# DMA transposes one block earlier, loads one chunk further ahead, and more half FFN steps as filler, in a fused attention and SwiGLU kernel

## The chip, the cores and the metric

The kernel runs on one core of a Trainium2 chip. The metric is device time in microseconds (us), the median of several executions. A program on one core has no second die to compare with, so a run counts as slow only if it is over 1.5% above the fastest run of the same kernel. Three different chips were used for the three rounds of experiments, and the kernel before was timed beside them each time; the median of its fast runs was 367.4, 368.1 and 369.65 us there. Absolute times are compared within one round, and ratios across rounds.

The readings call the engines by short names: PE (TensorE), PEld (its weight loads), DVE (VectorE), ACT (ScalarE), POOL (GpSimd), SP (SyncE, which here only issues DMAs). The granted clock is the share of full speed that the throttle of TensorE allowed, so 0.5 is half clock; a dip is a stretch in which it is below 1. A wait, a landing time or a start is that of the one execution that was profiled.

## The reference, cut to what matters

```python
# q, k, v: (8 batches, 8 heads, 576 positions, 64);  window 64, causal
scores = q @ k.T / 8;  masked to 0 <= i - j < 64;  softmax
attn_out = softmax(scores) @ v            # per batch and head
x = attn_out as (4608 tokens, 512)
g = x @ w_gate                            # 512 x 1536
out = (silu(g) * (x @ w_val)) @ w_out     # 1536 x 512
```

The kernel works in 36 chunks of 128 tokens for attention and 9 groups of 512 tokens (four chunks) for the FFN.

## The kernel before

Every operation is recorded in program order with what it reads and writes. The recorder then gives each engine its own queue in that order and adds semaphore waits for data (a write before a read) and for buffers (a read before the next write). DMAs are recorded on the queue of the engine that issues them: loads on GpSimd, transposes and output stores on SyncE. A queue is in order: a DMA that has to wait holds up those recorded after it.

In the code below the calls are abridged and "..." marks cuts; the line numbers are those that the profile gives.

```python
NQ = 6       # buffers for q and k chunks as loaded
NV = 10      # for v
NZ = 4       # buffers for transposed q (qT); kT keeps all chunks

def TD(self, n):                 # transposes of k and q of chunk n, by DMA
    g.op("sp", dma_start_transpose(kT[n], kn[n % NQ]), ...)      # L363
    g.op("sp", dma_start_transpose(qT[n % NZ], qn[n % NQ]), ...) # L366
def XD(self, n):                 # transpose of the attention output of chunk n
    g.op("sp", dma_start_transpose(xT[...], xb[n % 4]), ...)     # L490
def A(self, n, nxt):             # attention-value matmuls of n; S(nxt) in the middle
def S(self, n):                  # score matmuls of n: need kT[n], qT[n]   (L394)
def F(self, c, f, t0=0, t1=512): # one FFN step (128 of the 1536 columns) of group c
def O(self, c, u):               # output tile u of group c, its store on SP
def T(self, n):                  # transposes of k and q by the PE (first chunks), L350
...
    self.F(0, 4, 0, 256)
    for f in range(5):
        self.F(0, f, 256, 512)
    self.T(4)
    ...
    self.S(8)
    self.O(0, 0)

    def block(n):
        load(n + 4)              # q, k, v of chunk n+4, on POOL
        self.A(n, n + 1)
        self.XD(n)               # not for n = 11
        self.TD(n + 2)
    place = {(1, 1, 0): 8, (1, 1, 2): 9, (1, 2, 1): 10, (1, 3, 0): 11, ...}
    # (group, output tile, step) -> block; from group 3 on one block for each output tile
```

The softmax here doesn't subtract the row's maximum and nothing guards it: scores larger than these inputs give would overflow.

Of the kernel before, what the change touches and what calls it, by code (L numbers as in the profile page):

```python
# [10 lines left out]
NCH = T // 128  # L11
# [138 lines left out]
class _Kernel:  # L150
# [423 lines left out]
    def build(self):  # L574
        W = lambda a, b: (self.load_w("g", a, b), self.load_w("v", a, b))

        def load(n):
            if n < NCH:
                self.load_qk(n)
                self.load_v(n)  # L580

        self.first_loads()
        self.init()
        self.load_v(0)
        self.init_pool_a()
        self.load_v(1)
        self.init_mask(self.nmask, "nmask", -30000.0)
        W(0, 1)
        self.load_qk(2)
        W(1, 2)  # L590
        self.load_qk(3)
        self.load_v(2)
        self.load_v(3)
        W(2, 4)
        self.init_mask(self.mask, "mask", 0.0)
        self.init_va(4, self.NV, "pool")
        for f in range(4, 12, 2):
            W(f, f + 2)
        for n in range(4, 8):
            load(n)  # L600

        self.banks("a", [5, 6, 7, 4, 0, 1])
        self.warm(13)
        self.first_cast("k", None, "dve")
        self.first_cast("q", 0, "act")
        self.first_cast("q", 1, "dve")
        tk = self.first_T("k")
        tq = self.first_T("q")
        b0, b1 = self.bias(0), self.bias(1)
        self.warm(2)  # L610
        for n in range(2):
            self.first_ev("k", n, "dve", *tk)
            self.first_ev("q", n, "act", *tq)
        self.S(0, b0)
        self.S(1, b1)
        self.warm(4)
        self.A(0)
        self.warm(2)
        self.A(1)
        self.warm(1)  # L620
        self.X(0, "act")
        self.warm(3)
        self.X(1, "act")
        self.warm(2)
        self.banks("a", [5, 6, 7, 4])
        self.F(0, 0, 0, 256)
        self.F(0, 1, 0, 256)
        self.T(2, "dve")
        self.T(3, "dve")
        load(8)  # L630
        b2 = self.bias(2)
        self.S(2, b2)
        b3 = self.bias(3)
        self.S(3, b3)
        self.F(0, 2, 0, 256)
        self.A(2)
        self.A(3)
        self.F(0, 3, 0, 256)
        self.X(2, "act")
        self.X(3, "act")  # L640
        self.F(0, 4, 0, 256)
        self.load_wo(0, 6)
        self.load_wo(6, 12)
        load(9)

        for f in range(5):
            self.F(0, f, 256, 512)
        self.T(4)
        load(10)
        self.F(0, 5)  # L650
        self.S(4)
        self.T(5)
        load(11)
        self.F(0, 6)
        self.A(4, 5)
        self.F(0, 7)
        self.T(6)
        self.X(4, "act")
        self.F(0, 8)
        self.A(5, 6)  # L660
        self.F(0, 9)
        self.X(5, "act")
        self.T(7)
        self.F(0, 10)
        self.A(6, 7)
        self.TD(8)
        self.F(0, 11)
        self.X(6, "act")
        self.F(1, 0, 0, 256)
        self.A(7)  # L670
        self.TD(9)
        self.F(1, 1, 0, 256)
        self.F(1, 2, 0, 256)
        self.X(7, "act")
        self.F(1, 3, 0, 256)
        for f in range(4):
            self.F(1, f, 256, 512)
        self.S(8)
        self.O(0, 0)

        def block(n):
            if n >= NCH:
                return
            load(n + 4)
            self.A(n, n + 1 if n + 1 < NCH else None)
            if n != 11:
                self.XD(n)
            if n + 2 < NCH:
                self.TD(n + 2)

        place = {(1, 1, 0): 8, (1, 1, 2): 9, (1, 2, 1): 10, (1, 3, 0): 11,
                 (2, 0, 0): 12, (2, 1, 0): 13, (2, 1, 2): 14, (2, 2, 1): 15, (2, 3, 0): 16}
        for n in range(17, NCH):
            place[(n - 5) // 4, (n - 5) % 4, 0] = n
        for c in range(1, NFC):
            for u in range(int(c == 1), 4):
                late = c == NFC - 1 and u == 3
                for s in range(3):
                    if (c, u, s) != (1, 1, 0):
                        self.F(c, 3 * u + s)  # L700
                    if s != 1 and (c, u, s) in place:
                        block(place[c, u, s])
                    if s == 1 and not late:
                        self.O(c - 1, u)
                        if (c, u) == (1, 3):
                            self.X(11, "act")
                    if s == 1 and (c, u, s) in place:
                        block(place[c, u, s])
                if late:
                    self.O(c - 1, u)  # L710
        for u in range(3):
            self.O(NFC - 1, u)
        self.O_last(NFC - 1, 3)
        self.g.emit()
# [42 lines left out]
```

## Time and profile before

| | before |
|---|---|
| time, median (the four runs beside the changed kernel) | 369.46 us |
| span of the profiled run | 369.7 us |
| PE busy | 328.5 us, 89% |
| PE waiting for "DMA qT<-qn" | 23.1 us in 11 waits |
| PE waiting for the first k chunk to transpose itself (T(4)) | 2.8 us |
| mean granted PE clock | 0.982 |

From the page of the kernel before: busy time, then two rows of the span in 40 equal slices (9.2 us each), a digit being tenths.

```profile
PE 328.5 (89%) x3428; PEld 166.3 (45%) x3467; DVE 213.3 (58%) x459; ACT 138.9 (38%) x249; POOL 112.7 (30%) x151
...
PE   7986998856699766999999998999899999999997
...
PEclk9999999899699998999999999999999999999999
```

PE has holes between the seventh and the sixteenth slice (roughly 60 to 150 us), and the granted clock has dips in the same places. From 260 us on it is full.

The waits of PE in the kernel before (line and what it waited for: total us, number, longest):

```profile
PE ps L394 <- DMA qT<-qn: 23.1, 11, 4.3
...
PE ps L350 <- DMA kn<-in_k_dram: 2.8, 1, 2.8
```

L394 is S, L350 is T. Next, the timeline of PE (start, duration, group of instructions; in brackets the idle time before it and what ended it), at S(9), S(10), S(11), S(12) and the first FFN matmuls after the last of them:

```profile
65.93 0.54 PE L394 MATMUL ps<-qT,kT 64*64 64x128 bf16 x21 [2.13 <-DMA qT<-qn]
...
78.17 0.41 PE L394 MATMUL ps<-qT,kT 64*64 64x128 bf16 x21 [3.67 <-DMA qT<-qn]
...
86.78 0.41 PE L394 MATMUL ps<-qT,kT 64*64 64x128 bf16 x21 [1.64 <-DMA qT<-qn]
...
95.50 0.64 PE L394 MATMUL ps<-qT,kT 64*64 64x128 bf16 x24 [4.34 <-DMA qT<-qn]
...
96.70 1.49 PE L508 MATMUL ps<-xT,Wg 128*128 128x512 bf16 x3 [0.33 <-DVE rc L458]
97.98 1.91 PE L508 MATMUL ps<-xT,Wv 128*128 128x512 bf16 x4
```

Four waits of 2.1, 3.7, 1.6 and 4.3 us stand within 30 us. After the last, a group of three gate matmuls of 512 columns took 1.49 us instead of 0.81, and a group of four value matmuls 1.91 us instead of 1.03. The Trainium skill, "TensorE: Matmul & The Clock Gate", Part 1, says that the clock falls to half after an idle window of about 3.4 us, that the window runs freely, and that the number of slow matmuls therefore varies from run to run. This trace agrees in kind: the granted clock is 0.67 in the stretch 90 to 100 us.

The queue of SP in the same stretch shows why S(10) is late:

```profile
67.98 1.20 SPq L490 DMA_TRANSPOSE xT<-xb  x1
69.23 1.26 SPq L363 DMA_TRANSPOSE kT<-kn  x1
70.53 1.90 SPq L366 DMA_TRANSPOSE qT<-qn  x1
```

These are the x transpose of block 8, then the k and q transposes of chunk 10. The q transpose was issued from 70.5 us on and landed 7.5 us later (the landing time that the view of this tile gives for this window), which is when S(10) started, at 78.2 us. Block 9, which holds S(10), came straight after.

From 259.9 to 302.55 us, with no loads left, five chunks took 42.65 us: 8.53 us each is PE's own pace.

### The profile page before, as it was taken

The page shows a single profiled execution, that of the slowest core. Times are in us where ns is not written, and L with a number is a line of the kernel's source. Part 1 is how long each engine was busy: PE and PEld are TensorE (multiplying, and loading weights), DVE is VectorE, ACT ScalarE, POOL GpSimd, SP SyncE. Part 2 cuts the span into 40 slices and gives each one's busy share as a digit, 9 for nine tenths or more (in the row PEclk, how much of TensorE's full clock was granted, in tenths as well). Part 3 has the DMA queues.
Part 4 walks back from the last instruction along what each step waited for, and adds up shares of the span by engine and source line. Part 5 has one row for each costly group of instructions (what it writes and reads, how often), then busy time and mean ns, then how long its engine had stood idle before and what let it go on. Part 6 is the DMA issues. An engine that isn't in the chain of part 4 may idle for free.

```text
span 369.7 us, 8222 instructions
## 1 busy us (share of the span) xinstructions
PE 328.5 (89%) x3428; PEld 166.3 (45%) x3467; DVE 213.3 (58%) x459; ACT 138.9 (38%) x249; POOL 112.7 (30%) x151
## 2 busy tenths in 40 slices
PE   7986998856699766999999998999899999999997
PEld 3555556323344333444444444444444444444444
DVE  4455897355366643666666665666566666445530
ACT  2553854323143331443333433333334442232321
POOL 7999964222502242222222242222000000000000
PEclk9999999899699998999999999999999999999999
DMA  9999999999968999999999999999423221101003
GB/s 171 157 176 169 169 175 154 170 115 126 121 75 89 128 124 83 120 111 125 125 116 128 133 101 125 127 119 85 102 73 73 73 73 43 44 28 57 30 29 113
DMA packets 169909, 40.26 MB, mean 109 GB/s; under 512 B 156432, under 2 KB 165392, under 8 KB 169872
## 3 DMA queue, kind: packets, MB, share of 16 engines
q0 software_dynamic: 117312, 18.36, 72.0%
q1 hardware_dynamic: 51376, 20.72, 30.6%
q10 hardware_dynamic: 1184, 0.66, 0.6%
q8 instruction: 27, 0.44, 0.5%
q14 instruction: 10, 0.08, 0.1%
HBM read 37.75 MB, written 9.44 MB: 128 GB/s over the span
## 4 chain that ended last, share of the span: by engine, by line
PE 33%; issue 31%; POOL 19%; DMA 14%; SPq 1%; DVE 1%; ACT 0%; POOLq 0%
PE ps L508 19%; PE ps L532 12%; DMA qT<-qn 6%; POOL qn L263 6%; POOL va L325 5%; DMA va<-in_v_dram 5%; POOL kn L263 3%; DMA kn<-in_k_dram 3%; POOL Wg L331 1%; POOL Wv L331 1%; PE ps L443 1%; PE ps L394 1%; SPq L363 1%; PE ps L561 1%; SPq L490 1%
## 5 line engine op out<-in xcount | busy, mean ns | idle before, releaser
L516 DVE SCALAR_TENSOR_TENSOR uu<-sig,ps 128x512 bf16<-128x512 bf16 (+1 forms) x117 | 75.3, 644 | 99.4 <-ACT sig L514 98.9
L508 PE MATMUL ps<-xT,Wv 128*128 128x512 bf16 (+1 forms) x467 | 114.1, 367 | 0.1
L508 PE MATMUL ps<-xT,Wg 128*128 128x512 bf16 (+1 forms) x435 | 107.4, 367 | 5.8 <-issue 4.5
L532 PE MATMUL ps<-Wo,hT 128*128 128x512 bf16 x417 | 95.8, 380 | 0.3 <-issue 0.2
L514 ACT ACTIVATE sig<-ps 128x512 bf16<-128x512 f32 (+1 forms) x117 | 66.1, 565 | 61.4 <-PE ps L508 61.1
L518 DVE SCALAR_TENSOR_TENSOR hT<-uu,ps 128x512 bf16<-128x512 bf16 (+1 forms) x117 | 75.5, 645 | 4.6 <-PE ps L508 0.5
L263 POOL DMA_DIRECT2D qn<-in_q_dram x38 | 34.5, 922 | 134.1 <-DMA qT<-qn 133.9
L508 PEld LDWEIGHTS ps<-xT,Wv 128*128 128x128 bf16 x468 | 46.3, 99 | 49.4 <-issue 3.2
L532 PEld LDWEIGHTS ps<-Wo,hT 128*128 128x128 bf16 x420 | 41.2, 98 | 49.9 <-issue 1.0
L508 PEld LDWEIGHTS ps<-xT,Wg 128*128 128x128 bf16 x468 | 42.8, 99 | 42.3 <-issue 1.6
L404 ACT ACTIVATE pt<-ps 128x512 bf16<-128x512 f32 x72 | 38.9, 595 | 50.3 <-PE ps L394 50.3
L544 ACT ACTIVATE ost<-ps 128x512 f32<-128x512 f32 x35 | 20.9, 597 | 98.0 <-PE ps L532 98.0
L394 PE MATMUL ps<-qT,kT 64*64 64x64 bf16 (+1 forms) x864 | 16.4, 207 | 24.2 <-DMA qT<-qn 23.1
L325 POOL DMA_DIRECT2D va<-in_v_dram x40 | 36.5, 920 | 1.6 <-DVE ident L226 0.8
L263 POOL DMA_DIRECT2D kn<-in_k_dram x38 | 34.6, 915 | 2.8 <-DMA Wo<-in_moe_w_out_dram 2.8
L461 DVE TENSOR_TENSOR xb<-ps,rc 128x256 bf16<-128x256 f32 x72 | 30.5, 424 | 2.5
L458 DVE RECIPROCAL rc<-ps 128x4 f32<-128x4 f32 x72 | 12.5, 174 | 30.8 <-PE ps L443 30.6
L394 PEld LDWEIGHTS ps<-qT,kT 64*64 64x64 bf16 x864 | 13.1, 111 | 27.7 <-issue 17.8
L443 PE MATMUL ps<-va,pt 64*64 64x65 bf16 x1088 | 23.8, 198 | 0.4
L409 DVE TENSOR_TENSOR pt<-pt,mask 128x512 bf16<-128x512 bf16 x64 | 24.1, 416 | 0.2 <-ACT pt L404 0.2
L443 PEld LDWEIGHTS ps<-va,pt 64*64 64x64 bf16 x1088 | 16.9, 109 | 15.6 <-issue 12.1
L311 PE MATMUL ps<-wz 128*128 128x512 bf16 x25 | 8.0, 458 | 1.4 <-DVE wz L225 1.3
(44 smaller groups left out, 63.2 us busy)
## 6 DMA issues: line engine op xcount, KB each, us to landing
out_dram<-ost SPq DMA_DIRECT2D x35, 256.0 KB, 2.3
va<-in_v_dram POOLq DMA_DIRECT2D x32, 128.0 KB, 6.2
qn<-in_q_dram POOLq DMA_DIRECT2D x30, 128.0 KB, 4.0
kn<-in_k_dram POOLq DMA_DIRECT2D x30, 128.0 KB, 5.6
Wo<-in_moe_w_out_dram POOLq DMA_DIRECT2D x2, 768.0 KB, 13.8
Wg<-in_moe_w_gate_dram POOLq DMA_DIRECT2D x5, 256.0 KB, 6.7
Wv<-in_moe_w_val_dram POOLq DMA_DIRECT2D x5, 256.0 KB, 7.4
fq<-in_q_dram ACTq DMA_DIRECT2D x1, 512.0 KB, 6.3
```

What stands on the lines that cost most here:

```text
L263: self.g.op("pool", lambda e, d=d, a=a: e.dma_start(d, a), writes=ks, dma=True)
L325: g.op("pool", lambda e, d=d, a=a: e.dma_start(d, a), writes=ks, dma=True)
L394: r = e.matmul(sv[h][o:o + 64, c, q0:q1], self.kT[ps, c, kk:kk + 64], qT[ps, c, q0:q1], start=not biased, stop=not biased or c == 3 and kk ...
L404: g.op("act", lambda e, po=po, si=si: e.activation(po, si, ACTF.Exp, scale=SCALE), reads=[bk], writes=[pk])
L409: "dve", lambda e: e.tensor_tensor(po, po, m, ALU.mult), reads=[pk, "mask"], writes=[pk]))
L443: r = e.matmul(av[half][ws, j, :], pt[ks, h, ws], vv[ks, h, 0:65], start=key == q[0], stop=key == q[-1])
L461: g.op("dve", lambda e, xo=xo, rb=rb, a=av[half]: e.tensor_tensor(xo, a[:, :, 0:64], rb, ALU.mult), reads=[bk, ("rc", ir)], writes=[("xb", ...
L508: r = e.matmul(bank[:, 0:n], W[:, kk, f * 128:f * 128 + 128], xT[:, kk, t0:t1], start=(kk == 0), stop=(kk == NK - 1))
L514: g.op("act", lambda e: e.activation(sig[:, 0:n], G[:, 0:n], ACTF.Tanh, scale=0.5), reads=[gk], writes=[("sig", i)])
L516: g.op("dve", lambda e: e.scalar_tensor_tensor(uu[:, 0:n], sig[:, 0:n], 1.0, G[:, 0:n], ALU.add, ALU.mult), reads=[("sig", i), gk], writes ...
L518: g.op("dve", lambda e: e.scalar_tensor_tensor(hT[:, f, t0:t1], uu[:, 0:n], 0.5, V[:, 0:n], ALU.mult, ALU.mult), reads=[("uu", i), vk], wr ...
L532: r = e.matmul(OB[:, :], hT[:, f, 128 * u:128 * u + 128], self.Wo[:, f, :], start=(f == 0), stop=(f == NF - 1))
```

## The change

Its intent: give the DMA transposes of k and q one block more of lead (chunk n+3 in block n), load five chunks ahead instead of four, put one more FFN step in front of the first chunk that has to wait for its load, and use steps of half the tokens as filler. Blocks 8 and 9 move later to make room. The core of the diff:

```diff
-        self.warm(2)
...
         self.X(2, "act")
+        self.F(0, 4, 0, 256)
         self.X(3, "act")
-        self.F(0, 4, 0, 256)
+        self.F(0, 5, 0, 256)
...
-        for f in range(5):
+        for f in range(6):
             self.F(0, f, 256, 512)
         self.T(4)
... (the steps after it move up by one; load(12) recorded here; T(7) goes ahead of X(5); TD(8), TD(9) as before)
+        self.F(1, 0..5, 0, 256) around X(6), A(7), X(7)
-        for f in range(4):
+        for f in range(3):
             self.F(1, f, 256, 512)
         self.S(8)
+        self.TD(10)
         self.O(0, 0)
+        for f in range(3, 6):
+            self.F(1, f, 256, 512)
 
         def block(n):
-            load(n + 4)
+            load(n + 5)
             self.A(n, n + 1 if n + 1 < NCH else None)
             if n != 11:
                 self.XD(n)
-            if n + 2 < NCH:
-                self.TD(n + 2)
+            if n + 3 < NCH:
+                self.TD(n + 3)
 
-        place = {(1, 1, 0): 8, (1, 1, 2): 9, (1, 2, 1): 10, (1, 3, 0): 11,
+        place = {(1, 1, 2): 8, (1, 2, 0): 9, (1, 2, 1): 10, (1, 3, 0): 11,
```

More of the change, by code (lines that the diff above doesn't have):

```diff
@@ L649, in build @@
         load(10)
-        self.F(0, 5)
+        self.F(0, 6)
         self.S(4)
@@ L653, in build @@
         load(11)
-        self.F(0, 6)
+        self.F(0, 7)
         self.A(4, 5)
-        self.F(0, 7)
+        self.F(0, 8)
         self.T(6)
+        load(12)
         self.X(4, "act")
-        self.F(0, 8)
+        self.F(0, 9)
         self.A(5, 6)
-        self.F(0, 9)
+        self.F(0, 10)
+        self.T(7)
         self.X(5, "act")
-        self.T(7)
-        self.F(0, 10)
+        self.F(0, 11)
         self.A(6, 7)
         self.TD(8)
-        self.F(0, 11)
+        self.F(1, 0, 0, 256)
+        self.F(1, 1, 0, 256)
         self.X(6, "act")
-        self.F(1, 0, 0, 256)
+        self.F(1, 2, 0, 256)
         self.A(7)
         self.TD(9)
-        self.F(1, 1, 0, 256)
-        self.F(1, 2, 0, 256)
+        self.F(1, 3, 0, 256)
+        self.F(1, 4, 0, 256)
         self.X(7, "act")
-        self.F(1, 3, 0, 256)
-        for f in range(4):
+        self.F(1, 5, 0, 256)
+        for f in range(3):
             self.F(1, f, 256, 512)
         self.S(8)
+        self.TD(10)
         self.O(0, 0)
+        for f in range(3, 6):
+            self.F(1, f, 256, 512)
         def block(n):
@@ L698, in build @@
                 for s in range(3):
-                    if (c, u, s) != (1, 1, 0):
+                    if (c, u) != (1, 1):
                         self.F(c, 3 * u + s)
@@ L704, in build @@
                         self.O(c - 1, u)
-                        if (c, u) == (1, 3):
-                            self.X(11, "act")
                     if s == 1 and (c, u, s) in place:
                         block(place[c, u, s])
+                    if (c, u, s) == (1, 3, 1):
+                        self.X(11, "act")
                 if late:
```

## The prediction

> **What bounds it now.** TensorE, and its waits in one stage. The page gives PE 328.5 us busy of 369.7. After the last load (260 to 302 us) the PE timeline shows the ideal pace: 8.53 us per chunk of 128 tokens (three FFN steps at 1.73, one output tile at 2.6, attention 0.75). Before that, the waits view charges the score matmuls (S) with 23.1 us for "DMA qT<-qn" in 11 waits: chunks 9 to 12 (2.1, 3.7, 1.6, 4.3 us), 15 to 17 (1.7, 1.7, 4.3), then 0.4 to 1.5 four times. Another 2.8 us is the first PE transpose of chunk 4, waiting for kn until 34 us.
>
> Block n queues the x transpose, then the k and q transposes (TD) of chunk n+2, behind attention n; S(n+2) comes in the very next block. The SP timeline shows some 3.8 us of issue, then the q transpose lands in 4.1 us (median), up to 8 while loads are backlogged (57 to 78 us). So 9 to 12 us are needed where 3.5 to 8.5 are given.
>
> After three waits the granted clock fell (windows: 0.83 at 60 to 70, 0.67 at 90 to 100, 0.83 at 140 to 150 us). The Trainium skill, "TensorE: Matmul & The Clock Gate", Part 1, says that the array drops to half clock after an idle window of about 3.4 us; the trace agrees: after the two 4.3 us waits four matmuls took 1.3 to 1.9 us instead of 1.03. Estimated cost: 4 us.
>
> **What changes.** TD(n+3) in block n gives one block more: 8.5 us in the steady part, at least 6 in the cluster of blocks 8 to 11. No matmul columns are added. Three more steps in halves: DVE pays 4x0.42 against 2x0.69 us each, 0.9 us in all, where DVE is 88 to 96% busy but PE sets the pace. Two warm-up matmuls (0.4 us) go. The extra FFN step is 1.7 us of filler inside the 2.8 us wait; half a step fills 0.7 us between x transposes.
>
> **Critical path (estimates from the trace).**
> - Until S(8): 1 us gained (chunk 4 still lands near 34 us).
> - S(9), S(10): no wait. TD(11) follows block 8 and has about 7 us: I keep 2 to 3 us of wait at S(11), 0 to 1 at S(12). S(13), now at 106.5, comes near 92: 14 us gained.
> - Chunks 13 to 35: 8.8 us of waits, clock loss, and 0.2 to 0.4 us a block go: 196 us become 180 to 183.
> - The tail (67 us after the last S) is unchanged.
>
> Sum: span 339.5 to 343, against 369.7; the timed median lies 1.7 us under the span.
>
> **Predicted time: 341.5 us**, 8 in 10 between 336 and 350. Faster by over 2%: 0.96; within 2%: 0.03; slower: 0.01.
>
> **What would show it.** Right: S waits for qT fall from 23.1 to under 5 us, the rest near chunks 11 and 12; mean granted clock rises from 0.98 to 0.99 or more; chunks 13 to 35 pace at 8.5 to 8.65 us; the chunk 4 wait falls to 1 to 2.2 us. Wrong: waits on kn loads at the SP queue or S, TD landings of 10 us or more, FFN steps of group 2 waiting for x transposes, or DVE holding banks at 45 to 65 us.
>
> **What would make it wrong.** DMA is at nine tenths until 260 us; if it has no room for a 4 to 5% faster pace, waits return as late loads: 348 to 355. If landing at 60 to 80 us stays at 8 us, S(11) and S(12) cost 3 us more and a clock dip.

## The result, and the profile after

The changed kernel took 347.38 us (median of four fast runs, 346.56 to 348.78) against 369.46 us. The ratio is 0.9407, with a 95% interval of 0.9337 to 0.9478. A ratio is the mean time of one kernel's fast runs over that of the other's in the same rounds, so it is not quite the ratio of the medians. The time lies in the predicted range, 5.9 us above the predicted value.

The page of the changed kernel, the same lines:

```profile
PE 330.0 (95%) x3489; PEld 166.4 (48%) x3489; DVE 212.6 (61%) x465; ACT 139.2 (40%) x252; POOL 112.7 (32%) x151
...
PE   6986998994999999999999999999999999999996
...
PEclk9999899997899999999999999999999999999999
```

One deep hole is left at the tenth slice (78 to 87 us), and one at the fourth (26 to 35 us). The waits of PE:

```profile
PE ps L394 <- DMA qT<-qn: 5.1, 1, 5.1
PE ps L350 <- DMA kn<-in_k_dram: 3.0, 1, 3.0
```

Ten of the eleven waits are gone. One of 5.1 us is left, and the wait of T(4) is no shorter than before. The timeline of PE at S(11) and what follows:

```profile
78.71 0.32 PE L443 MATMUL ps<-va,pt 64*64 64x65 bf16 x16
84.15 0.63 PE L394 MATMUL ps<-qT,kT 64*64 64x128 bf16 x22 [5.12 <-DMA qT<-qn]
...
84.94 1.89 PE L508 MATMUL ps<-xT,Wg 128*128 128x512 bf16 x4
86.62 1.91 PE L508 MATMUL ps<-xT,Wv 128*128 128x512 bf16 x4
88.33 1.57 PE L508 MATMUL ps<-xT,Wg 128*128 128x512 bf16 x4
89.74 1.03 PE L508 MATMUL ps<-xT,Wv 128*128 128x512 bf16 x4
```

The wait is followed by slow matmuls: three groups of four took 1.89, 1.91 and 1.57 us where 1.03 is normal. So S(11) cost about 7.4 us in all (5.1 of wait and 2.3 of half clock).

Where the time went, stage by stage, from the start of the score matmuls of three chunks in each profiled run (the last column is the end of the span; the two lower rows are experiments that are told below):

| | S(8) | S(13) | S(35) | end |
|---|---|---|---|---|
| before | 60.4 | 106.5 | 302.55 | 369.7 |
| changed | 62.0 | 99.6 | 279.85 | 347.1 |
| transposes moved alone | 62.3 | 94.3 | 274.5 | 341.7 |
| changed, loads from chunk 15 held | 62.3 | 92.7 | 273.4 | 340.6 |

Up to S(8) the change lost 1.6 us. From S(8) to S(13) it took 37.6 us instead of 46.1. From S(13) to S(35) it took 180.3 instead of 196.1, and PE was busy for 179.9 of that. The tail of 67.2 us stayed. The large gain is where it was predicted, in the even part; the stage of chunks 9 to 12 gave 8.5 us where about 13 was forecast (46 us down to 33, from S(8) at 59.4 to S(13) at 92).

### The profile page after: what moved, and what is told of

It reads as the page before. It is cut to its first block, busy times and chain, and to the rows that moved or that the text cites. A ratio compares the mean times of both kernels' runs of the same rounds, so it can differ in the third digit from the quotient of the medians.

```text
span 347.1 us, 8322 instructions
## 1 busy us (share of the span) xinstructions
PE 330.0 (95%) x3489; PEld 166.4 (48%) x3489; DVE 212.6 (61%) x465; ACT 139.2 (40%) x252; POOL 112.7 (32%) x151
## 4 chain that ended last, share of the span: by engine, by line
PE 75%; POOL 11%; DMA 10%; issue 3%; DVE 0%; ACT 0%; POOLq 0%
PE ps L508 45%; PE ps L532 24%; DMA qn<-in_q_dram 5%; PE ps L443 3%; POOL va L325 3%; DMA kn<-in_k_dram 3%; DMA qT<-qn 2%; POOL kn L263 2%; PE ps L394 2%; POOL qn L263 2%; POOL Wv L331 2%; POOL Wg L331 2%; PE ps L561 1%; POOL Wo L336 0%; POOL nmask L251 0%
## 5 line engine op out<-in xcount | busy, mean ns | idle before, releaser
L508 PE MATMUL ps<-xT,Wg 128*128 128x512 bf16 (+1 forms) x480 | 115.6, 364 | 0.9 <-DVE uu L516 0.6
L508 PEld LDWEIGHTS ps<-xT,Wv 128*128 128x128 bf16 x480 | 47.2, 99 | 48.5 <-issue 2.2
L508 PEld LDWEIGHTS ps<-xT,Wg 128*128 128x128 bf16 x480 | 44.1, 99 | 42.5 <-issue 2.2
L443 PE MATMUL ps<-va,pt 64*64 64x65 bf16 x1088 | 23.0, 197 | 0.6 <-DVE pt L409 0.2
L443 PEld LDWEIGHTS ps<-va,pt 64*64 64x64 bf16 x1088 | 15.3, 107 | 15.8 <-issue 11.2
```

The lines of the kernel that those rows point to most:

```text
L443: r = e.matmul(av[half][ws, j, :], pt[ks, h, ws], vv[ks, h, 0:65], start=key == q[0], stop=key == q[-1])
L508: r = e.matmul(bank[:, 0:n], W[:, kk, f * 128:f * 128 + 128], xT[:, kk, t0:t1], start=(kk == 0), stop=(kk == NK - 1))
```

## The experiments

Theory A: the gain comes from the transposes' lead alone, and what is missing in the stage of chunks 9 to 12 is a late landing of the transposes of chunk 11. Rival B: the fillers and the load distance make part of the gain. For the shortfall there were two rivals: C, the transposes of chunk 11 are issued too late because block 8 was moved back; D, they are slowed by other DMA traffic.

### Loads four ahead again (e3), and the changed kernel a second time (e11)

```diff
-        load(12)
...
-            load(n + 5)
+            load(n + 4)
```

> The changed kernel with loads issued four chunks ahead as before. Built, it gives the same instructions with the same waits on every engine as the changed kernel, since GpSimd's queue holds the same loads in the same order and a load is held by its buffer, not by its place in the program. So if that reading is right it is a second sample of the changed kernel: 346 to 349 us, ratio to before 0.94, S(11) waiting about 5 us. If the load distance mattered it would be slower by several us.

Measured: 347.0 us (344.65 to 348.0, six runs), ratio 0.9448 (0.9408 to 0.9489). The built program has the same instructions in the same order with the same waits on every engine as the changed one (apart from source line numbers the two programs are equal). So the phrase "loads five" names no change to the machine: a load on POOL is held by its ring buffer, which comes free when TD of the chunk six earlier has landed, and not by its place in the program.

> The changed kernel itself, so that the other two are compared with it on one chip: 346 to 348.5 us.

Measured: 347.51 us (344.8 to 348.84), ratio 0.9418 (0.9364 to 0.9472). These two and the first measurement are three samples of one program: 347.0 to 347.5 us on three occasions. Single runs spread by 4 us, and their mean granted clock lies between 0.985 and 0.995. The profile of e3 shows a source of the spread: there the wait of T(4) was 2.69 us, no dip followed, and S(8) came at 60.06 us instead of 62.02.

### The transposes alone (e1), and everything else alone (e2)

e1, against the kernel before:

```diff
         self.S(8)
+        self.TD(10)
         self.O(0, 0)
...
-            if n + 2 < NCH:
-                self.TD(n + 2)
+            if n + 3 < NCH:
+                self.TD(n + 3)
```

> The kernel before, with the DMA transposes three chunks ahead and nothing else changed. Lead theory: waits of S for qT fall from 23.1 us to under 7 (chunk 9 keeps about 2), and the time to 347 to 353 us. Filler theory (the order of FFN steps makes the gain): over 360 us.

e2 is the changed kernel with these three lines undone:

> The changed kernel with the DMA transposes only two chunks ahead, all fillers and the new places of blocks 8 and 9 kept. Lead theory: the waits for qT are back, 20 us or more, and since block 9 now comes one FFN step after block 8 S(10) alone waits 6 us or more; 366 to 376 us. Filler theory: under 358 us.

Measured on the same chip and in the same rounds as e3: e1 343.39 us, ratio 0.9359 (0.932 to 0.9399); e2 367.62 us, ratio 1.0035 (0.9988 to 1.0081), with 17.6 us of waits for qT, a little under the 20 that I had expected; S(10) waited 4.9 us, not 6 or more. e1 was better than I had expected, and 3.6 us faster than the changed kernel's program (e3). All of the gain is the transposes' lead. The fillers and the new places of blocks 8 and 9 gain nothing by themselves, and beside the lead they cost 3 to 4 us. Rival B falls.

The waits of PE in e1, first T(4), then S:

```profile
PE ps L350 <- DMA kn<-in_k_dram: 3.4, 1, 3.4
...
PE ps L394 <- DMA qT<-qn: 0.5, 1, 0.5
```

Only 0.5 us is left at S, so the hole at S(11) belongs to the arrangement and not to the lead. T(4) waits 3.4 us here against 3.0 in the changed kernel, and S(8) came at 62.3 us against 62.0, both with a clock dip behind T(4). No gain from the sixth step in front of T(4) can be read from this: in three profiles of the changed kernel's own program S(8) came at 60.06 (e3), 62.02 and 62.29 us (e11).

### Chunk 11 issued earlier (e4)

```diff
         self.TD(10)
+        self.TD(11)
...
-            if n + 3 < NCH:
+            if n != 8 and n + 3 < NCH:
```

> The changed kernel with the transposes of chunk 11 issued beside those of chunk 10, ahead of attention 8, instead of behind it. If the one wait of 5.1 us at S(11) and the clock dip behind it (about 2.4 us) come from the late issue: the wait is gone, S(12) waits under 1.5 us, 339.5 to 342.5 us, mean clock 0.99 or more. If the DMA engines' backlog is the bound, the wait moves to S(12) or to the x transposes and the time stays above 345 us.

Measured: 346.34 us (344.08 to 346.88), ratio 0.9421 (0.9381 to 0.9462): no gain over e3's 347.0 beyond the spread. The wait at S(11) is gone, but S(12) waits 3.1 us instead (in the profiled run, one of the two fastest at 344.64 us), since now the transposes of chunk 12 landed 8.3 us after the start of their issue. My first expectation failed; the outcome is the second one's, that the wait moves on. An earlier issue of one transpose only hands the delay to the next, so C alone does not explain the shortfall.

### The loads held out of the burst (e5)

The timeline of SP in the changed kernel, from the two output stores to the transposes of chunk 12:

```profile
65.82 5.54 SPq L546 DMA_DIRECT2D out_dram<-ost  x2
72.92 1.21 SPq L490 DMA_TRANSPOSE xT<-xb  x1
74.17 1.27 SPq L363 DMA_TRANSPOSE kT<-kn  x1
75.49 1.33 SPq L366 DMA_TRANSPOSE qT<-qn  x1
76.86 1.52 SPq L490 DMA_TRANSPOSE xT<-xb  x1
78.42 2.44 SPq L363 DMA_TRANSPOSE kT<-kn  x1
80.91 1.28 SPq L366 DMA_TRANSPOSE qT<-qn  x1
```

And of POOL in the same stretch:

```profile
65.81 0.88 POOL L263 DMA_DIRECT2D qn<-in_q_dram  x1 [4.88 <-DMA qT<-qn]
66.67 0.89 POOL L263 DMA_DIRECT2D kn<-in_k_dram  x1
67.53 0.90 POOL L325 DMA_DIRECT2D va<-in_v_dram  x1
69.37 0.88 POOL L263 DMA_DIRECT2D qn<-in_q_dram  x1 [0.94 <-DMA qT<-qn]
70.24 0.88 POOL L263 DMA_DIRECT2D kn<-in_k_dram  x1
71.10 0.89 POOL L325 DMA_DIRECT2D va<-in_v_dram  x1
84.35 0.88 POOL L263 DMA_DIRECT2D qn<-in_q_dram  x1 [12.36 <-DMA qT<-qn]
```

At 65.8 us the transposes of chunk 9 have landed and at 69.4 us those of chunk 10. Each landing frees a q and k buffer, and so the loads of chunks 15 and 16 go out at once, just before the transposes of chunk 11 (74.2 and 75.5 us). In the kernel before the load of chunk 16 went out only at 78.4 us, because chunk 10 was transposed later; that of chunk 15 went out at 66.1 us there too. So the change itself has brought one of the two loads forward, by 9 us. The load at 84.35 us, of chunk 17, waited for the landing of chunk 11 in the same way. The q transpose of chunk 11 took 8.6 us from the start of its issue to landing. e5 holds the loads from chunk 15 on until the transposes of chunk 12 have landed:

```diff
     def load_qk(self, n):
+        hold = [self.last_td] if n == 15 else []      # last_td: the q transpose of chunk 12
...
-                self.g.op("pool", lambda e, d=d, a=a: e.dma_start(d, a), writes=ks, dma=True)
+                self.g.op("pool", lambda e, d=d, a=a: e.dma_start(d, a), writes=ks, dma=True, after=hold)
```

> The changed kernel, where the loads of chunk 15 and of all later chunks wait until the transposes of chunk 12 have landed (in the changed kernel the loads of 15 and 16 are issued at 66 to 72 us, into the burst). If these loads slow the transposes of chunk 11 (8.7 us from the start of the q issue to landing), it lands within 6 us, S(11) waits under 2.5 us instead of 5, and the time is 341 to 345 us. If the burst is slow by itself (four k and q transposes, two x transposes and two outputs on one queue, behind the loads up to chunk 14), S(11) still waits 4 us or more and the time stays at 345.5 to 349 us.

Measured: 341.45 us (341.39 to 342.33, six runs), ratio 0.9284 (0.9232 to 0.9336). The q transpose of chunk 11 landed 3.4 us after its issue began, at nearly the same moment of the program (75.7 us against 75.5), and that of chunk 12 after 2.5 us. From the view of the tile qT, in a window that holds this one transpose, in the changed kernel and then in e5:

```profile
L366 SPq DMA_TRANSPOSE qT<-qn x1: 1327/1327/1327, 75.5 to 75.5; - x1
...
DMA to landing us min/median/max: 8.6/8.6/8.6
```

```profile
L367 SPq DMA_TRANSPOSE qT<-qn x1: 2137/2137/2137, 75.7 to 75.7; - x1
...
DMA to landing us min/median/max: 3.4/3.4/3.4
```

S(11) waited for no DMA at all, only 0.44 us for an eviction by ACT (from the PE timeline of e5):

```profile
79.73 0.41 PE L395 MATMUL ps<-qT,kT 64*64 64x128 bf16 x22 [0.44 <-ACT ost L545]
```

The busy time by stretch, in the changed kernel and then in e5 (columns: stretch and length, busy time and number of instructions of PE, PEld, DVE, ACT and POOL, granted clock, DMA share, GB/s; I read a share above 1 as packets of several queues that overlap in time):

```profile
73.00:79.00 6.00, 5.85 (x87) 2.71 (x84) 4.83 (x12) 2.10 (x5) 0.00 (x0) 1.00 2.09 180
79.00:85.00 6.00, 0.88 (x45) 0.82 (x42) 0.00 (x0) 0.56 (x2) 0.65 (x1) 0.80 1.66 129
```

```profile
73.00:79.00 6.00, 5.69 (x75) 2.65 (x74) 5.09 (x13) 2.18 (x4) 0.00 (x0) 1.00 1.05 135
79.00:85.00 6.00, 5.25 (x130) 3.04 (x132) 4.37 (x11) 3.47 (x7) 1.68 (x2) 1.00 0.53 132
```

From 73 to 79 us the share is 2.09 with the loads and 1.05 without. From 79 to 85 us PE is busy 0.88 us of 6 with them and 5.25 without. The Trainium skill, "DMA: Bandwidth & Descriptors", section "Issuing engines are not separate DMA queues", says that DMAs from all queues run on the same 16 engines and interleave; this run shows what that costs here: 3.4 us becomes 8.6. Rival D is shown for the two loads together; which of them does how much was not tried. In the same rounds e7, the changed kernel with one step more in front of T(4), took 346.03 us. The later loads lost nothing by the hold: no S after it waited over 0.25 us for its transposes.

### Block 8 at its old place (e6)

```diff
         self.O(0, 0)
-        for f in range(3, 6):
-            self.F(1, f, 256, 512)      # moved behind block 8
...
-        place = {(1, 1, 2): 8, (1, 2, 0): 9, (1, 2, 1): 10, (1, 3, 0): 11,
+        place = {(1, 1, 0): 8, (1, 1, 2): 9, (1, 2, 1): 10, (1, 3, 0): 11,
```

> The changed kernel with attention blocks 8 and 9 in their places of before: block 8 straight after the first output tile of group 0, the three upper halves of FFN steps 3 to 5 after it. If the move of block 8 costs the changed kernel its 3.5 us against the transposes alone: no wait at S(11), 342 to 344 us. If the halves in the preamble cost it: 346 us or more.

Measured: 343.49 us (342.14 to 344.61), ratio 0.9333 (0.9277 to 0.9389), with no wait for a DMA at S(11); S(9) waited 2.5 us. The first expectation holds, and the ratio is near e1's (0.9359). With block 8 early the transposes of chunk 11 are issued 5 us earlier, and their slow landing (7.5 us, from 70.6 us) is over before S(11) comes at 81.1 us. So the wait at S(11) needs both, the move of block 8 and the two loads: e5 takes away the loads alone, e6 the move alone, and each removes it. The move took away the slack, and the loads used the rest up.

### A seventh step in front of T(4) (e7), and with block 8 back (e8)

```diff
         for f in range(6):
             self.F(0, f, 256, 512)
+        self.F(0, 6)
         self.T(4)
... (the later steps move up by one; T(7), F(0, 11), X(5) in this order)
```

> The changed kernel with a seventh FFN step ahead of the transpose of chunk 4. Its wait for kn falls from 3 us to 1 to 1.6, and the clock dip behind it is gone. If S(11) is timed by the PE's own order the whole gain of 2 to 3 us arrives: 343.5 to 345.5 us. If the transposes of chunk 11 land when the DMA engines have worked off their backlog, whatever PE does, S(11) waits longer by what was gained: 346 to 348 us.

> Both of the last two: blocks 8 and 9 at their old places and seven FFN steps ahead of chunk 4. If each removes its own loss: no wait over 1.5 us at any S, the chunk 4 wait 1 to 1.6 us, 339.5 to 342 us, mean clock 0.995 or more. If the backlog sets the pace up to chunk 12, the gain of one is lost again at S(9) to S(12): 342.5 to 345 us.

Measured: e7 346.03 us, ratio 0.941 (0.936 to 0.946); e8 343.99 us, ratio 0.9358 (0.9304 to 0.9411). T(4) waited 0.9 and 1.1 us, with no dip behind it, and yet e8 is no faster than e6 in the same rounds. Two things stood against the gain. The missing filler between A(5) and T(7) opened a new wait of 1.5 us at T(7), for a PSUM bank (a part of the memory that PE writes its results to) that the DVE was still reading. And S(9) waits for its transposes when PE comes early: it started at 66.4, 66.1 and 66.2 us in e1, e6 and e8, although S(8) had come at 62.3, 60.2 and 59.8. Both times lie in the ranges of the second expectations. But the longer wait at S(11) that was expected with it in e7 is not there: it was 4.7 us, as in e3.

### Both measures together (e9), and the hold without the fillers (e10)

e9 is the changed kernel with the hold of e5 and a seventh step, where F(0, 11) is cut in halves around T(7). e10 is e1 with the hold of e5.

> Candidate for the best: the changed kernel with the loads from chunk 15 on held until the transposes of chunk 12 have landed, and with a seventh FFN step ahead of chunk 4 (the eleventh step in halves around the transpose of chunk 7, against the bank wait of 1.5 us that the first try of seven steps had there). Against loads held alone (341.5 us): the chunk 4 wait falls from 3.3 to about 1.2 us and its clock dip (1.7 us) goes: 338 to 340 us. If what is gained before chunk 9 is lost again in waits at S(9) to S(12), as with both earlier runs of seven steps: 340.5 to 342.5 us.

> The transposes alone moved in the kernel before, with the loads from chunk 15 on held as well. There block 8 comes early enough that a slow landing (8.4 us at chunk 11) is covered, with only 0.5 us of wait at S(12). If the loads matter only where the time between issue and use is short, this changes under 1 us: 342.5 to 344 us. If they slow the stage in some other way, it gains 2 us or more like the changed kernel.

Measured beside e11 (347.51 us) on one chip: e9 342.68 us, ratio 0.9284 (0.923 to 0.9337); e10 343.52 us, ratio 0.9311 (0.9262 to 0.9361). e9 missed its first expectation and lies 0.2 us above the range of the second, whose mechanism it shows. S(8) came at 59.2 us, 3 us earlier than in e5, and S(11) then waited 2.9 us. Although no load was issued between 62 and 80 us, the q transpose of chunk 11 landed 6.3 us after the start of its issue, at 79.0 us; in e5, issued 3 us later, it landed at 79.1. And in e10, issued at 70.9 us, it took 7.8 us and landed at 78.7, with the loads held as well. I read that as the backlog of the loads up to chunk 14, which is worked off at about that time; no run took those loads away, so this is not shown. e10 came out as its first expectation said: where the lead covers a slow landing, holding the loads changes nothing clear of noise.

The traces of e1 and e10 also bound what the two loads do. They added little to the landing of a q transpose issued at 70.8 us (8.1 us in e1, 7.8 with the loads held), but much to one issued at 78.0 (7.5 against 3.0). So they are not why transposes issued from 58 to 71 us land slowly (7.3 to 7.8 us in e10 too); they keep landings slow for those issued later. S(11) of the changed kernel, whose q transpose was issued at 75.5 us, fell into that extension.

e5 and e9 are the best versions, with the same ratio to the kernel before, 0.9284. e9 beats the changed kernel by 4.8 us on the same chip; e5 was not run beside it, but its interval (up to 0.9336) lies below those of e3 (from 0.9408) and e11 (from 0.9364).

## Why the prediction was right or wrong

- **What bounds the kernel: right.** 23.1 us of waits of S fell to 5.1 (forecast: under 5), and e1 and e2 show that the transposes' lead did it, alone.
- **Chunks 13 to 35: right.** Predicted 180 to 183 us, measured 180.3; from S(17) (126.5 us) to S(35) it is 8.52 us a chunk. The DMA engines had room for the faster pace.
- **The tail: right.** 67.2 us in both.
- **S(9) and S(10) without waits for DMA: right.** They waited 0.4 us at most, for an eviction by ACT.
- **S(11): the step that failed, by its size.** The prediction kept "2 to 3 us of wait at S(11)". It was 5.1 us, with 2.3 us of half clock behind it, about 5 us more than forecast, and with it S(13) came at 99.6 us instead of 92. In the prediction's own terms 9 to 12 us are needed and TD(11) "has about 7": from the x transpose behind block 8 (72.9 us) to the landing (84.1) it needed 11.2 us, and it had 6.1 until PE was ready (79.0). I took landing times from the trace of before (4 to 8 us, the long ones put down to a backlog that would be over), and did not ask what the earlier landing of chunk 10 would set free. It set free the load of chunk 16, 9 us earlier than before; with the load of chunk 15, which went out at 66 us in both kernels, e5 shows it to be worth 8.6 against 3.4 us of landing. The warning stood in the prediction's last paragraph, as a risk of 3 us and a dip; it should have been in the sum.
- **Until S(8): wrong in sign.** Predicted 1 us gained; measured 1.6 us lost. "The chunk 4 wait falls to 1 to 2.2 us" failed: it was 3.05 us, because PE also reached T(4) with less work before it, and chunk 4 was there only at 34.5 us instead of 33.9. The warm-up matmuls were gone, the first data came 0.6 us earlier and the gaps between the x transposes were filled. So PE arrived at 31.4 us instead of 31.1, in spite of 1.7 us more filler. In the profiled run a clock dip of about 1.6 us followed; in e3 it did not, and there S(8) came 0.35 us earlier than before. Another 0.85 us went where PE waited for DVE around 54 us (0.25 and 0.6 us), which the prediction had listed among the signs of being wrong.
- **The clock: nearly right.** It rose from 0.982 to 0.985 in the profiled run, and to 0.985 or 0.99 in all four runs of the result, against "0.99 or more".
- **The load distance** is not costed in the prediction, which does not mention it. e3 shows that it is no change at all.
- **Time and span: a slip.** The prediction puts the timed median 1.7 us under the span. Each run's time lies 1.7 us above its own span (348.78 against 347.1 in the profiled run). The predicted 341.5 is about the middle of the predicted spans; as a time the same sum comes to about 343.

The sum of the two misses, 2.6 us until S(8) (62.0 against 59.4) and 5.0 us from there to S(13), is more than the 5.9 us by which the time was off; the rest of the span came out at the low end of its forecast.

## What to carry to other kernels

Before moving a transfer forward, follow its landing one step further: which buffer does it free, which transfer waits for that buffer, and into what will that one collide? Ring buffers pass an earlier landing on as an earlier load, and here two loads that were not needed for another 30 us more than doubled the landing time (3.4 to 8.6 us) of a transfer that was needed in 4; here one extra dependency held it back at no cost. And test the parts of a bundled change alone: here three lines, the lead of the transposes, were the whole gain, one part was no change to the built program, and the rest cost about 15% of the gain (3.6 of 24.0 us).

## What the Trainium skill lacked or had wrong

- "Advanced Engine Details and Errata", "X-Bar Transpose (TRN2)", says that transpose DMAs are as fast as regular ones. By landing time these runs do not contradict it: in e5 at 80 to 82 us a transpose of 128x512 bf16 landed in 2.5 us and an output store of 256 KB in 2.4 us, and in the changed kernel, where the q transpose issued at 75.5 us took 8.6 us, the loads of 128 KB issued from 65.8 to 71.1 us took 11.0 to 14.4. What the section does not say is that a transpose costs its queue more: in the changed kernel the issue of one held SP for 1.19 to 2.44 us, that of an output store of 256 KB for 0.33 to 0.59 us.
- "DMA: Bandwidth & Descriptors", "Issuing engines are not separate DMA queues", says that DMAs from all queues interleave, and "Latency and other measured facts" on the same page gives an HBM access latency of 2 us at high load. Neither gives a figure for what one queue's traffic adds to another queue's transfer: here six loads of 128 KB each raised the landing time of a transpose from 3.4 to 8.6 us (e5 against the changed kernel), and that of one issued at 70.8 us hardly at all (7.8 to 8.1 us, e10 against e1).
- "TensorE: Matmul & The Clock Gate", Part 1, gives idle windows of about 3.4 us as the condition of a fall to half clock. Two waits shorter than that were followed by slow matmuls (2.1 us in the kernel before, 3.05 us in the changed one), a third was not (2.69 us in e3), and neither was one that is longer (3.7 us in the kernel before). The page does say that the window runs freely, but a threshold on one wait is not what these traces show.
